# Retention, PReLU layer and routed experts in one kernel: a shift of float64 low bits moves from VectorE to ScalarE, and the planner counts other durations

## The chip, the cores and the metric

One NeuronCore of a Trainium2 chip runs the whole program. It has five engines that this document speaks of: TensorE (PE, and PEld for its weight loads), VectorE (DVE), ScalarE (ACT), GpSimd (POOL) and SyncE (SP, which issues most transfers). Each engine takes its instructions strictly in the order in which they were issued to it. The metric is the device time of one execution in microseconds (us).

## The reference, cut to what matters

Three layers follow one another. The sizes are 4 sequences of 768 tokens, 8 heads of 64 columns, so 3072 tokens of 512 columns.

```
state = gamma[h] * state + k_t v_t^T          # retention, per head; y_t = q_t state / sqrt(64)
h = x @ w_in                                  # 512 x 2048
g = max(h, 0) + alpha * min(h, 0)
x = (g @ w_out).astype(float32)               # 2048 x 512
logits = unit(x) @ unit(expert_emb).T / tau   # 8 experts, the best one is taken
out = gate * (max(x @ w1[e], 0) @ w2[e])      # 512 x 1024 and 1024 x 512
```

`w_in` and `w_out` are float64, because the draw of float32 numbers is multiplied by `1.0 / np.sqrt(...)` of NumPy's float64. The kernel gets them as the 64-bit patterns that they are.

## The kernel before, in words

**Tiles and stages.** A token tile is 128 tokens; there are 24, tile i being chunk i // 4 of sequence i % 4. Four tiles form a block. Products are done in float16 halves (a value is split into a high and a low half, and three products replace one), scaled by powers of two. The program has these stages:

1. The start: retention of tiles 0 to 7, the float64 weights `w_in` to float32 and then to halves.
2. The hidden layer of block 0 (`mm1(0, m)` for 16 values of m), and beside it the rest of `w_in`, all of `w_out`, and retention of four more tiles.
3. A long loop over steps: for each block the second product of the layer (`mm2`), the next block's `mm1`, the remaining retention tiles, the routing of finished tiles, and the splitting of the experts' weights into halves that go back to DRAM (`half_load`, `half_scale`, `half_pair`).
4. The routed experts' layer, slot by slot of 128 tokens of one expert.

**The conversion.** `convert(w, g, src)` turns a pair of chunks, 128 x 1024 float64 numbers, into float32. There are 16 pairs, eight of `w_in` and eight of `w_out`. A pair lands in one of three buffers that are used in turn (`f64_ring`, two parts of `f64_buf` and one of `pay_buf`), as pairs of 32-bit words, or four 16-bit words `h[:, :, 0..3]` a number, lowest first. On this follow:

- ScalarE multiplies the high word, read as a float32, by 2^-112 into `x`.
- VectorE shifts `h[:, :, 1]` right by 13 and writes the three bits into `h[:, :, 0]`.
- VectorE takes the sign out of `h[:, :, 3]` and writes it into `h[:, :, 1]`.
- VectorE shifts the bits of `x` left by 3 and puts in the low 32-bit word `f[:, :, 0]`, which now holds the sign and the three bits.
- ScalarE squares `x` and adds it up (`square_sum`), with the buffer `f` as the place for the squares, which nobody reads. After that the buffer takes the next pair.

The sums of squares give the scales, and `quarter(q)` and `split_out(g)` split the float32 chunks into halves on ScalarE and on VectorE or GpSimd in turn.

**The order of the work.** The kernel's text does not set the order directly. A class `Plan` records every instruction, with what it reads and writes, an engine and a duration in ns from `cost()`. `issue()` then works out, back from the end, by when each one is needed, plays the program through with these durations and the hand-over times of `AFTER`, and lets each engine take, of the instructions that are ready, the one that is needed first. The order found so is what is issued, on all five engines. It is fixed when the program is built; nothing of it is decided on the chip. Every recorded instruction is called at one line, 145, so most rows of the trace have that line, and the tiles tell them apart.

The changed lines are in `cost()` (lines 158 to 181 before) and `convert()` (lines 619 to 636).

Of the kernel before, what the change touches and what calls it, by code (L numbers as in the profile page):

```python
# [12 lines left out]
I32 = mybir.dt.int32  # L13
U16 = mybir.dt.uint16
AF = mybir.ActivationFunctionType
# [5 lines left out]
E, F = 8, 1024  # L21
P = 128
NCH = S // P              # chunks of a sequence
NTILE = NT // P           # token tiles: tile i is chunk i // B of sequence i % B
BT = B                    # token tiles of a block: one chunk of each sequence
# [4 lines left out]
NPRE = 2                  # tiles of the expert that has most tokens before the last block  # L30
NMIN = NTILE - NPRE       # the other tiles of tokens sorted by expert, at least
NSLOT = NMIN + E - 1      # and at most
SL = 30
CAP = NT                  # rows of an expert's region
PW = DM + 2               # words of a routed token: hi | lo | gate | id
# [3 lines left out]
# Powers of two that bring a norm into [2^(C-190.5), 2^(C-189.5)).  # L39
# [6 lines left out]
# columns of the float32 constants  # L46
# [11 lines left out]
def _constants():  # L58
# [23 lines left out]
    # decay of a query and of a key, by chunk: [c, (h2 d), 2, pair, t]  # L82
# [13 lines left out]
class Plan:  # L96
    """Records instructions in the order in which they would be right one after the other, and
    issues them in one in which each engine always takes, of the instructions whose operands are
    there, the one that is needed first. An instruction's place in the tensor engine's own
    sequence, and what waits for it, say when it is needed."""  # L100

    # from the end of an instruction to the start of another that waits for it; a DMA's issue
    # and its transfer are apart
    AFTER = {"PE": 197.0, "ACT": 145.0, "DVE": 140.0, "POOL": 100.0, "SP": 0.0}
    DMA_DONE, DMA_RATE = 940.0, 360.0
    COLD = 1500.0, 3500.0        # the tensor engine's idle time after which it is slow, and for how long
    SLACK = 8000.0
    PATIENCE = 0.7, 2000.0
    AHEAD = 60000.0          # how long before it is needed a DMA may be issued
    BACKLOG = 2500.0         # of DMA, beyond which none is issued  # L110

    def __init__(self, nc):
        self.nc = nc
        self.nodes = []
        self.log = {}            # reads and writes of a tensor: (region, node)
        self.unit_ = None
        self.pe_time = 0.0
        self.bias = 0.0
        self.vector = self.Engine(self, nc.vector, "DVE")
        self.scalar = self.Engine(self, nc.scalar, "ACT")  # L120
        self.gpsimd = self.Engine(self, nc.gpsimd, "POOL")
        self.tensor = self.Engine(self, nc.tensor, "PE")
        self.sync = self.Engine(self, nc.sync, "SP")
# [9 lines left out]
    class Engine:  # L133
# [23 lines left out]

        def cost(self, method, kw):
            """Engine's time, time until the result is there, bytes moved."""
# [16 lines left out]
            if self.name == "ACT":  # L176
                return 30.0 + 0.9 * n + (90.0 if kw.get("accum_out") is not None else 0.0), 0.0, 0
            if self.name == "DVE":
                fast = method in ("tensor_scalar", "tensor_copy") and n > 64
                return 65.0 + n * (0.52 if fast else 1.05), 0.0, 0  # L180
# [48 lines left out]
    def unit(self, eng):  # L229
        """Instructions of one engine that stay together."""  # L230
# [16 lines left out]
    def issue(self):  # L247
# [19 lines left out]
        while True:  # L267
# [16 lines left out]
            # rather wait a little for what is needed earlier  # L284
# [35 lines left out]
def retention_prelu_moe_kernel(ctx: ExitStack, tc, qkv, w_in, w_out, alpha, emb, tau, w1, w2,  # L320
# [17 lines left out]
    class Ring:  # L338
        """Buffers used in turn."""
# [28 lines left out]
    # A matrix in float32 lies two chunks of 512 columns behind the place where its halves go,  # L368
    # so that a pair's halves never land on what is still to be split.
    win = buf("win", [KF + 2, 512])  # L370
    wout = buf("wout", [KF + 2, 512])
    stage = buf("stage", [16, 512])         # experts' weights; before, halves of g
    xT = [buf(f"xT{k}", [2, KD, BW], F16) for k in range(2)]
    st_bd = buf("st_bd", [B, KD, P])
    f64_buf = buf("f64_buf", [4, 512, 2], I32)   # float64 weights; later, halves of g
# [7 lines left out]
    # the first chunk's tiles use what else waits for w_out  # L383
# [34 lines left out]
    def pow2(ss, s, c, hb=None):  # L418
        """Powers of two by which vectors of squared norm ss are scaled, into s."""
# [10 lines left out]
    def total(acc, n):  # L430
        """Sum of acc over partitions and columns, on every partition."""
        ps = m_ring.next()
        T.matmul(out=ps[:, 0:n], lhsT=ones32, rhs=acc, start=True, stop=True)
        t = tmp("tot", [1])
        V.tensor_reduce(out=t, in_=ps[:, 0:n], axis=AX.X, op=ALU.add)
        return t
# [4 lines left out]
    def norm(ss, n, e):  # L441
        """Newton's steps on 1/sqrt; 1e-6 on top of the norm."""
# [15 lines left out]
    def split(hi, lo, src, s, pool):  # L458
        """Halves of a pair of chunks. For the Pool engine the chunks are scaled first."""
# [21 lines left out]
    def att_hat(i):  # L481
        """Decayed queries and keys of tile i."""
# [11 lines left out]
    def att_a(i):  # L494
        """Masked scores of tile i."""
        hat = att[i]
        ring = x_ring if i < B + N_EARLY else m_ring
        # heads of one half of the partitions share a bank
# [14 lines left out]
    # From tile HALVED on, scores and values go into their product as halves.  # L513
# [8 lines left out]
    def att_s(i):  # L522
        """Halves of the scores and values of tile i; the state, scaled as their product is."""
# [27 lines left out]
    def att_b(i, early=False):  # L551
        """Outputs of tile i, the state after it, the halves of x."""
# [48 lines left out]
    def att_x(i, src):  # L601
        """The halves of x with the model dimension on partitions."""
# [4 lines left out]
    # The exponent is rebased by a product that moves the high word's upper eight exponent  # L607
    # bits, which takes what is too small for float32 to zero.
# [4 lines left out]
    s_in = buf("s_in", [KD])        # a scale for every quarter of w_in's columns  # L613
    i_in = buf("i_in", [KD])
    s_g = buf("s_g", [KD])          # what the halves of w_out's rows of a quarter are scaled by
# [3 lines left out]
    def convert(w, g, src):  # L619
        """Pair g of chunks to float32."""  # L620
        f = f64_ring.next()
        # w_in's chunks in the order of its columns
# [8 lines left out]
        # the low word becomes the sign and the three bits that the high word's shift makes room for  # L631
        h = f.rearrange("p n t -> p (n t)").bitcast(U16).rearrange("p (n t) -> p n t", t=4)
        V.tensor_scalar(out=h[:, :, 0], in0=h[:, :, 1], scalar1=13, scalar2=None, op0=ALU.logical_shift_right)
# [4 lines left out]
    def alpha_bound():  # L638
        # |g| <= |h| sqrt(1 + sum over partitions of their largest alpha^2)
# [7 lines left out]
    def quarter(q):  # L647
        """Halves of a quarter of w_in's columns."""
# [88 lines left out]
    class Route:  # L737
# [7 lines left out]
        def halve(self, o, acc):  # L745
            """A routed token's row: the halves of x scaled, its gate, where it is from."""
# [24 lines left out]
        def finish(self):  # L771
# [6 lines left out]
            # 1 / scale of the row; over the norm, for the logits  # L778
# [14 lines left out]
            # the first of the largest  # L793
# [7 lines left out]
            # ranks  # L801
# [17 lines left out]
            # gates  # L819
# [39 lines left out]
    g16 = {}  # L859

    def mm1(j, m):
# [11 lines left out]
        if j == 0:  # L873
            # the Pool engine takes a part while the vector engine has most to do
# [32 lines left out]
    # slots: the two tiles known early, what there is at least, what there may be  # L907
# [41 lines left out]
    def gather(t):  # L949
# [4 lines left out]
        # with the model dimension on partitions  # L954
# [78 lines left out]
    LAG = 0, 2, 4, 5          # of a tile's second layer in the last block  # L1033
# [52 lines left out]
    # the first slot's tokens  # L1086
# [11 lines left out]
    # the tiles that are left  # L1098
# [3 lines left out]
    # tiles of experts up to each one  # L1102
# [5 lines left out]
    # even slots take tiles from the first on, odd slots from the last back  # L1108
# [29 lines left out]
    # where a slot has no token, one that surely is there is read in its place, and nothing written  # L1138
# [8 lines left out]
    # expert of each slot; whether its weights have to be loaded  # L1147
# [11 lines left out]
    # 1 / (S_w1 S_w2) of each slot  # L1159
# [16 lines left out]
    def load_w(t):  # L1176
        """Weights of a slot, or of the two early ones. A slot's stay for the next but one of the same expert."""
        for piece in range(4):
# [3 lines left out]
            if t in (0, 1):  # L1182
                # the first of all tiles, and the last
# [93 lines left out]
def _arrange(inputs):  # L1277
    """The inputs as the chip loads them: each partition's share of a load in one run."""
    q, k, v = inputs["q"], inputs["k"], inputs["v"]

    def by_dim(a):      # [b, h, s, d] -> [(c b), (h2 d), (pair t)]
# [3 lines left out]
    def by_token(a):    # [b, h, s, d] -> [(c b), t, (h d)]  # L1285
# [5 lines left out]
    def rows(a):        # [.., (k p), f] -> [.., p, (k f)]  # L1291
# [4 lines left out]
    def in_chunks(a):  # L1296
# [5 lines left out]
        # float64, handed over as the bits that it is  # L1302
# [29 lines left out]
```

## Time and profile before

| | |
|---|---|
| median of 3 runs | 1041.25 us (1040.83 to 1045.32) |
| profiled execution, span from first to last instruction | 1051.0 us (its time with what lies around the span is not listed) |
| mean granted TensorE clock | 0.960 of full |
| busy, share of the span | PE 90%, PEld 53%, DVE 54%, ACT 47%, POOL 29% |
| instructions | 19041 |
| moved by the DMA engines | 201.45 MB, mean 192 GB/s |

The profiled execution is one execution, with its own start and end; its span is compared with stretches of its own trace, and the runs with one another. "Busy" is the time that an engine spends in instructions other than waits, branches and the issue of transfers. The page cuts the span into 40 slices of 26.3 us and gives the busy share of each in tenths (9 is 90% or more). A wait is put down to the instruction that came last of those it waited for.

### The profile page before, as it was taken

Reading aid. Unit: us, or ns where it says so; the run is one execution under the profiler, and the core shown is the slowest. Engines: PE = TensorE matmul, PEld = TensorE weight load, DVE = VectorE, ACT = ScalarE, POOL = GpSimd, SP = SyncE. Lnnn points to the kernel's source line nnn. Section 1 sums busy time; section 2 is a strip of 40 time slices with the busy share of each in tenths; the row PEclk is TensorE's granted clock in tenths of the full one; section 3 lists DMA queues with packets and bytes.
Section 4 is the critical chain, followed back from the end, with each engine's and each line's share of the span. In section 5 each row is a group of like instructions: output and inputs, shape, how many; then the busy total and the mean of one; then the engine's idle time right before and its main releaser. Section 6 shows DMA issues by size and latency. Waiting matters only on the chain. (4 is left out here: it accounts for less than half of the span.)

```text
span 1051.0 us, 19041 instructions
## 1 busy us (share of the span) xinstructions
PE 943.4 (90%) x7100; PEld 561.8 (53%) x7100; DVE 570.0 (54%) x1299; ACT 492.6 (47%) x865; POOL 304.0 (29%) x316
## 2 busy tenths in 40 slices
PE   5778876999999988988999899899889999998995
PEld 5664543555554544444444444444677777775763
DVE  5999999546766775567345554645712222221231
ACT  1457666546767956787667658742101010100100
POOL 1234556312342433323312321440231212113110
PEclk9887788999999989999999999999999999999998
DMA  8986532463866956876476557569575399825670
GB/s 279 307 268 193 189 129 71 114 188 91 234 197 197 251 151 213 240 201 191 171 220 164 187 181 214 157 219 316 186 201 168 72 292 315 243 65 132 151 287 21
DMA packets 129824, 201.45 MB, mean 192 GB/s; under 512 B 89726, under 2 KB 90110, under 8 KB 124608
## 3 DMA queue, kind: packets, MB, share of 16 engines
q1 hardware_dynamic: 123168, 179.42, 58.1%
q0 software_dynamic: 6560, 20.77, 5.8%
q8 instruction: 57, 0.93, 0.4%
q14 instruction: 39, 0.32, 0.1%
HBM read 204.59 MB, written 51.14 MB: 243 GB/s over the span
## 5 line engine op out<-in xcount | busy, mean ns | idle before, releaser
L145 PE MATMUL bank<-xT,win 128*128 128x512 f16 (+1 forms) x2208 | 338.9, 310 | 14.5 <-ACT g L145 7.3
L145 PEld LDWEIGHTS <-win 128*128 128x128 f16 x2400 | 186.8, 100 | 153.8 <-issue 31.9
L145 PE MATMUL bank<-wout,f_buf 128*128 128x512 f16 x960 | 227.5, 384 | 5.6 <-DVE pay_buf L145 4.8
L145 PEld LDWEIGHTS <-f_buf 128*128 128x128 f16 x960 | 92.9, 99 | 115.6 <-issue 11.4
L145 ACT ACTIVATE stage<-stage 128x1024 f16<-128x1024 f32 x96 | 101.0, 1052 | 54.9 <-DMA wsplit<-stage 46.0
L145 POOL TENSOR_TENSOR stage<-stage 128x1024 f16<-128x1024 f32 x32 | 68.2, 2131 | 146.1 <-ACT stage L145 117.8
L145 DVE SCALAR_TENSOR_TENSOR f_buf<-g,f_buf 128x512 f16<-128x512 f32 x80 | 72.7, 909 | 53.1 <-ACT f_buf L145 52.9
L145 DVE SCALAR_TENSOR_TENSOR g<-g,oma,bank 128x512 f32<-128x512 f32 x80 | 59.4, 744 | 73.5 <-ACT g L145 73.3
L145 ACT ACTIVATE st_bd<-bank 128x512 f16<-128x512 f32 x30 | 17.9, 597 | 149.7 <-PE bank L145 129.6
L145 POOL DMA_INDIRECT out<-xT,ids x25 | 25.3, 1013 | 214.4 <-DVE xT L145 181.5
L145 ACT ACTIVATE stage<-stage,se 128x1024 f16<-128x1024 f32 (+1 forms) x64 | 71.6, 1139 | 11.2 <-DVE se L145 6.5
L145 POOL TENSOR_TENSOR hat_buf<-qk_buf,cqk_sb 128x512 f32<-128x512 f32 x32 | 46.4, 1452 | 83.4 <-DMA qk_buf<-in_qkv 44.9
L145 PEld LDWEIGHTS <-wout 128*128 128x128 f16 x1152 | 65.5, 98 | 7.8 <-issue 4.8
L145 ACT ACTIVATE g<-bank 128x512 f32<-128x512 f32 x96 | 55.9, 584 | 26.0 <-PE bank L145 25.9
L145 PE MATMUL bank<-xT,wout 128*128 128x128 f16 x1056 | 62.7, 219 | 3.5 <-issue 3.4
L145 ACT ACTIVATE f_buf<-g 128x512 f16<-128x512 f32 x80 | 49.8, 622 | 34.1 <-DVE g L145 34.1
L145 PEld LDWEIGHTS <-st_bd 128*128 128x128 f16 x408 | 39.7, 99 | 45.3 <-issue 1.6
L145 DVE SCALAR_TENSOR_TENSOR st_bd<-bank,st_bd 128x512 f16<-128x512 f32 x34 | 23.5, 690 | 65.7 <-ACT st_bd L145 58.5
L145 DVE TENSOR_SCALAR xT<-bank,f_buf,cqk_sb 128x512 f32<-128x512 f32 x22 | 17.8, 809 | 67.0 <-PE bank L145 67.0
L145 PE MATMUL bank<-win,st_bd 128*128 128x512 f16 x216 | 49.4, 386 | 0.0
L145 PE MATMUL bank<-wout,stage 128*128 128x512 f16 (+1 forms) x208 | 48.8, 388 | 0.0
L145 DVE SCALAR_TENSOR_TENSOR stage<-stage,se 128x1024 f16<-128x1024 f32 x32 | 41.1, 1283 | 12.4 <-ACT stage L145 11.0
(253 smaller groups left out, 1320.9 us busy)
## 6 DMA issues: line engine op xcount, KB each, us to landing
win<-wsplit SPq DMA_DIRECT2D x56, 1024.0 KB
wout<-wsplit SPq DMA_DIRECT2D x52, 1024.0 KB
stage<-in_w SPq DMA_DIRECT2D x64, 512.0 KB
wsplit<-stage SPq DMA_DIRECT2D x64, 512.0 KB
qk_buf<-in_qkv SPq DMA_DIRECT2D x18, 768.0 KB
f_buf<-in_w_in SPq DMA_DIRECT2D x12, 512.0 KB
vp_buf<-in_qkv SPq DMA_DIRECT2D x20, 256.0 KB
f_buf<-in_w_out SPq DMA_DIRECT2D x10, 512.0 KB
```

Source lines behind the costliest of these rows:

```text
L145: call = lambda: fn(**kw)
```

## The change

In `convert`, ScalarE writes the three bits instead of VectorE, as a number: the 16-bit word times 2^-13, plus 2^-14 - 0.5, which rounded to an integer is the word shifted right by 13. The result is written as a whole 32-bit word, so that `h[:, :, 1]` is cleared by it, and VectorE's next step, which writes the sign there, comes after it. In `cost()` the durations of ScalarE and VectorE change. ScalarE's depend on where the input lies and on operands that are columns in memory; VectorE's no longer count operations on bits as fast ones, and count long instructions with two inputs 15% longer. Comments and docstrings go as well.

```diff
@@ cost()
+        BITS = (ALU.logical_shift_right, ALU.logical_shift_left, ALU.bitwise_and, ALU.bitwise_or)
+
         def cost(self, method, kw):
...
             if self.name == "ACT":
-                return 30.0 + 0.9 * n + (90.0 if kw.get("accum_out") is not None else 0.0), 0.0, 0
+                extra = sum(93.0 for k in ("accum_out", "scale", "bias") if isinstance(kw.get(k), bass.AP))
+                return (95.0 if kw["in_"].space != bass.MemoryType.PSUM else 50.0) + 0.833 * n + extra, 0.0, 0
             if self.name == "DVE":
-                fast = method in ("tensor_scalar", "tensor_copy") and n > 64
-                return 65.0 + n * (0.52 if fast else 1.05), 0.0, 0
+                fast = method in ("tensor_scalar", "tensor_copy") and n > 64 and kw.get("op0") not in self.BITS
+                two = method in ("scalar_tensor_tensor", "tensor_tensor") and n > 256
+                return 65.0 + n * (0.52 if fast else 1.05) * (1.15 if two else 1.0), 0.0, 0
             return 140.0 + (2.13 if method == "tensor_tensor" else 1.3) * n, 0.0, 0
@@ convert()
         A.activation(out=x, in_=f[:, :, 1].bitcast(F32), func=AF.Copy, scale=2.0 ** -112)
         h = f.rearrange("p n t -> p (n t)").bitcast(U16).rearrange("p (n t) -> p n t", t=4)
-        V.tensor_scalar(out=h[:, :, 0], in0=h[:, :, 1], scalar1=13, scalar2=None, op0=ALU.logical_shift_right)
+        A.activation(out=f[:, :, 0], in_=h[:, :, 1], func=AF.Copy, scale=2.0 ** -13, bias=2.0 ** -14 - 0.5)
         V.tensor_scalar(out=h[:, :, 1], in0=h[:, :, 3], scalar1=0x8000, scalar2=None, op0=ALU.bitwise_and)
         V.scalar_tensor_tensor(out=b, in0=b, scalar=3, in1=f[:, :, 0], op0=ALU.logical_shift_left, op1=ALU.bitwise_or)
```

## Rows read from the trace of the kernel before

**Rows 1.** The page: busy us by engine, then busy tenths in 40 slices.

```profile
PE 943.4 (90%) x7100; PEld 561.8 (53%) x7100; DVE 570.0 (54%) x1299; ACT 492.6 (47%) x865; POOL 304.0 (29%) x316
...
PE   5778876999999988988999899899889999998995
...
DVE  5999999546766775567345554645712222221231
```

**Rows 2.** Windows: stretch, length, busy us of each engine, granted clock, DMA share, GB/s.

```profile
20.00:181.00 161.00, 124.27 (x748) 84.85 (x748) 155.54 (x215) 95.57 (x156) 74.06 (x47) 0.85 0.63 193
...
20.00:80.00 60.00, 45.16 (x328) 38.30 (x327) 57.34 (x87) 29.07 (x50) 17.83 (x12) 0.88 0.88 262
...
181.00:1051.00 870.00, 809.12 (x6295) 467.68 (x6294) 404.75 (x1064) 394.08 (x707) 227.56 (x263) 0.98 0.64 188
240.00:700.00 460.00, 427.80 (x2493) 210.50 (x2492) 271.95 (x642) 323.46 (x574) 145.37 (x183) 0.98 0.65 193
400.00:500.00 100.00, 89.42 (x573) 45.77 (x572) 61.47 (x152) 74.29 (x138) 32.22 (x38) 0.98 0.72 206
500.00:600.00 100.00, 94.36 (x484) 43.44 (x482) 48.12 (x105) 65.12 (x106) 24.20 (x33) 1.00 0.63 186
```

**Rows 3.** Waits of VectorE, 20 to 181 us: total us, times, longest.

```profile
DVE hbx L145 <- ACT wout L145: 1.5, 3, 0.6
DVE g L145 <- ACT g L145: 1.2, 1, 1.2
DVE st_bd L145 <- PE bank L145: 0.8, 1, 0.8
```

**Rows 4.** Waits of TensorE, 20 to 181 us.

```profile
PE bank L145 <- DVE xh L145: 10.1, 3, 6.5
...
PE bank L145 <- ACT g L145: 7.3, 2, 6.6
```

**Rows 5.** Waits of ScalarE, 20 to 181 us.

```profile
ACT stage L145 <- DVE g L145: 14.9, 9, 2.9
```

**Rows 6.** VectorE's groups, 20 to 181 us: busy us, mean ns, idle before.

```profile
L145 DVE TENSOR_SCALAR f_buf<-f_buf 128x1024 uint16<-128x1024 uint16 x22 | 34.6, 1573 | 0.1
...
L145 DVE TENSOR_SCALAR pay_buf<-pay_buf 128x1024 uint16<-128x1024 uint16 x10 | 16.9, 1693 | 0.0
```

**Rows 7.** Timeline of VectorE: start us, duration us, instruction.

```profile
52.03 1.30 DVE L145 TENSOR_SCALAR pay_buf<-pay_buf 128x1024 uint16<-128x1024 uint16 x1
53.12 1.35 DVE L145 TENSOR_SCALAR f_buf<-f_buf 128x1024 uint16<-128x1024 uint16 x1
54.28 1.34 DVE L145 TENSOR_SCALAR pay_buf<-pay_buf 128x1024 uint16<-128x1024 uint16 x1
...
71.03 2.37 DVE L145 TENSOR_SCALAR pay_buf<-pay_buf 128x1024 uint16<-128x1024 uint16 x1
```

**Rows 8.** Timeline of GpSimd at the same time.

```profile
70.81 3.57 POOL L145 TENSOR_TENSOR hat_buf<-qk_buf,cqk_sb 128x512 f32<-128x512 f32 x2 [0.25 <-DMA cqk_sb<-in_cqk]
```

**Rows 9.** Timeline of ScalarE.

```profile
47.70 1.15 ACT L145 ACTIVATE win<-pay_buf 128x1024 f32<-128x1024 f32 x1
48.73 0.69 ACT L145 ACTIVATE wout<-bank,sx 128x512 f16<-128x512 f32 x1
```

**Rows 10.** ScalarE's groups, 20 to 181 us.

```profile
L145 ACT ACTIVATE win<-f_buf 128x1024 f32<-128x1024 f32 x6 | 6.8, 1132 | 0.0
...
L145 ACT ACTIVATE win<-win,s_in 128x1024 f16<-128x1024 f32 x4 | 4.6, 1146 | 3.7 <-DVE s_in L145 3.7
...
L145 ACT ACTIVATE win<-win 128x1024 f16<-128x1024 f32 x4 | 4.2, 1057 | 4.3 <-DVE win L145 4.3
```

**Rows 11.** One tile, `f_buf`: duration ns min/median/max, first and last start.

```profile
L145 SPq DMA_DIRECT2D f_buf<-in_w_in x12: 327/328/572, 6.8 to 97.0; - x12
...
L145 ACT ACTIVATION_READ_ACCUMULATOR f_buf<-wout x5: 186/187/221, 70.7 to 156.9; 128x1 f32 x5
```

**Rows 12.** Groups of the whole span: VectorE's costliest.

```profile
L145 DVE SCALAR_TENSOR_TENSOR f_buf<-g,f_buf 128x512 f16<-128x512 f32 x80 | 72.7, 909 | 53.1 <-ACT f_buf L145 52.9
```

## The prediction

> **What bounds the kernel now.** I read the page first: TensorE is busy for 90% of the span, VectorE for 54%, ScalarE for 47% [rows 1]. These are averages over two different stages, as the 40 slices show: in slices 2 to 7 VectorE stands at 9 tenths or more and TensorE at 6 to 8, and from slice 8 on it is the other way round [rows 1]. So the second view is the table of windows [rows 2]. From 20 to 181 us VectorE is busy for 155.5 of 161 us (97%), TensorE for 124.3, so it is idle for 36.7 us, and ScalarE for 95.6, so idle for 65.4. From 181 us to the end TensorE is busy for 809.1 of 870 us and VectorE for less than half.
>
> The third view says who waits for whom between 20 and 181 us. VectorE waits for 1.5, 1.2 and 0.8 us, and that is all [rows 3]. TensorE waits most for VectorE (10.1 us for the halves of x in xh), and the 7.3 us that are put down to ScalarE's g [rows 4] lie behind VectorE too, because ScalarE itself stands 14.9 us in front of its copies of g until VectorE has made them [rows 5]. So in this stage VectorE sets the end, and it has no gap left. The page's chain of what ended last tells only of the end of the kernel and is of no help here. All 16 conversions of float64 pairs lie in this stage, with 32 VectorE instructions on 128x1024 16-bit words [rows 6].
>
> The runs listed have a median of 1041.25 us; the profiled execution has a span of 1051.0 us, 9.75 us (0.9%) above it, and what lies around that span is not listed by itself. I make the sum on the profiled execution and take the difference over to the median unscaled.
>
> **The change part by part.** *Removed: 16 shifts on VectorE.* The two groups of 16-bit instructions hold 34.6 and 16.9 us in 32 instructions, 1.61 us each, and half of them go: 25.8 us by their durations [rows 6]. That is the upper bound. Two such instructions in a row start 1.09 and 1.16 us apart though each lasts 1.3 (at 52.03, 53.12 and 54.28 us) [rows 7], because the end of one overlaps the start of the next; 16 x 1.1 = 17.6 us is the lower bound. Most of the rest is waiting beside GpSimd: the one at 71.03 us lasts 2.37 us [rows 7] while GpSimd runs two products from 70.81 to 74.38 us [rows 8]. Whether such a wait goes with the instruction or falls on the next one is open. Of the excess, 51.5 - 32 x 1.31 = 9.6 us, half belongs to the shifts; I let half of that go: 17.6 + 2.4 = 20 us off VectorE.
>
> *A rule that speaks against the change.* The trace has VectorE at 1.1 us per 1024 words between starts [rows 7], and ScalarE at 1.03 us, from 47.70 to 48.73 us, for a copy that reads the same buffer [rows 9]: the two are level. The Trainium skill (ScalarE: Activation LUTs, section Rules for kernel authors) would keep a multiply or an add on VectorE, up to about three times as fast per element there. If that held, a shift would be worth some 0.35 us, the relief an estimated 16 x 0.35 = 5.6 us, and the result 1036 us at best. The row decides against it, since these words lie four apart and pass at about one in 1.07 ns, so this gets no chance of its own.
>
> *Two readings of the port.* VectorE's instruction is lengthened beside GpSimd's [rows 7, 8]. The Trainium skill (SBUF — State Buffer, section Who interferes with whom) lets those two share a pair of ports that one instruction holds to its end, with ScalarE never waiting for anyone. By it the moved instruction leaves the lock for good, and the sum would go by the 25.8 us instead of 20: some 1020 us.
>
> *Added: 16 products on ScalarE.* The trace has none with 16-bit input and 32-bit output at this stride. The nearest row is the copy that reads the same buffer with the same step, 1.13 us; a dense one takes 1.06 us [rows 10]. Below, 16 x 1.06 = 17 us; above, if the strided write cost as much again as the whole, 16 x 2.1 = 34 us. I take 1.13, 18.1 us in all. They lie in ScalarE's 65.4 idle us of the stage and leave 47, so I cost them at nothing; if that cover were gone they would cost their 18 us.
>
> *Added: a wait.* Before, VectorE could do both 16-bit steps as soon as a pair had landed. Now the mask writes the halfword that the product reads, so it waits for ScalarE, 16 times, and everything behind it on VectorE (the masked scores, g, the halves of x) waits too, since the order is fixed, and TensorE behind that. Lower bound 0, where the product comes early enough; upper bound 16 times the longest wait of VectorE for ScalarE in the stage, 1.2 us, 19 us. The ordinary wait of that kind is 0.5 us (1.5 in three) [rows 3]; with two thirds of the masks caught by one I take 5 us.
>
> *Held buffers.* The pairs go through three buffers. The first load is issued at 6.8 us and the last square sum over a pair is read at 156.9 us [rows 11]; 16 pairs on three buffers are 5.33 turns, so a turn lasts about 28 us, most of it queueing on VectorE, which shrinks with VectorE's load. I cost nothing, and a rival stands on the opposite. The DMA engines are busy for 0.88 of the time from 20 to 80 us, 0.63 over the stage [rows 2]; no long wait of VectorE is for a load [rows 3], so this costs nothing in the forecast, though it caps what the first 60 us can gain.
>
> *The planner's durations.* They add and remove no instruction; they change the order on every queue, SP's and GpSimd's too. A bit operation on 1024 columns counted 597 ns and counts 1140 (traced 1.1 us between starts); a two-input one on 512 counted 603 and counts 683; a scaled copy of 1024 on ScalarE counted 952 like an unscaled one and counts 1041, and the trace has 1146 against 1057 for these [rows 10]. In the first stage the plan had taken VectorE for lighter than it is by 32 x 0.5 = 16 us. For the stage that TensorE bounds I can only bound the effect. TensorE's busy time in two neighbouring windows of 100 us with the same loops is 89.4 and 94.4 us [rows 2], 5 us apart, so plus or minus 2.5 us in 100; over the 460 us from 240 to 700 that is 11.5 us either way. I take 0, having no row for a direction.
>
> *Sum.* 20 us off VectorE, less 5 us of new waits, takes 15 us off the stage from 20 to 181 us, which then lasts 146. TensorE's 124.3 busy us fit into that (85%). Its granted clock, 0.85 over the stage [rows 2], may rise when its gaps shrink; as VectorE sets the stage I count nothing for it. What follows is bound by TensorE and simply begins 15 us earlier: span 1036, and for the runs 1041.25 - 15 = **1026 us**. What is late next is still VectorE, up to about 166 us.
>
> **The rivals.** *The new hand-over eats the relief.* The masks wait about 1 us each, near the longest that VectorE now waits, and the waits beside GpSimd fall on other instructions: 17.6 - 16 = 1.6 us gained, 1039 to 1040 us. For it: the two engines already wait for one another in turn, 14.9 us before the copies of g alone [rows 5]. Against it: ScalarE is idle for two fifths of the stage.
>
> *The order gets worse where TensorE bounds.* The 15 us come, and 11.5 are lost again from 240 to 700 us: 1038 us. For it: every queue is reordered, by numbers of which the two-input one (683 ns) still misses the 909 ns of its costliest group [rows 12]. Against it: the new numbers are mostly nearer to the rows.
>
> *The three buffers become the bound; slower than before.* A turn needs one more ScalarE step in series (1.03 us and a hand-over of some 0.2), and that step stands in ScalarE's fixed order behind instructions that wait for VectorE, up to 2.9 us each (14.9 us in 9 waits is 1.7 on average) [rows 5]. The relief is worth 3 x 1.1 = 3.3 us a turn. From about 2 us of such queueing for each pair on, a turn is longer than before; at 4 us it is 1.03 + 0.2 + 4 - 3.3 = 1.9 us longer, 5.33 turns give 10 us, and the time is 1051 us. For it: the serial chain. Against it: the 28 us of a turn are mostly queueing on the engine that is relieved.
>
> *The new durations help beyond the first stage.* 15 and most of 11.5 us: 1016 us or less.
>
> **How the numbers follow.** Forecast 0.60 (1017 to 1034 by itself), hand-over 0.10, worse order 0.10, buffers 0.12, more than forecast 0.08. The range reaches from 25.8 us of relief with no new wait and half of the planner's gain (1041.25 - 25.8 - 5.5 = 1010) to a little above no change (1043), which takes in the two middle rivals with a small loss. About 0.5% (5.2 us) is what a measurement of this kernel tells from no change. Faster by more than that: the forecast, the larger gain and 0.04 of the worse order, whose loss may be smaller, 0.72; within it: the rest of the two middle rivals, 0.16; slower: 0.12.
>
> **What would show it.** After: 16 instead of 32 16-bit instructions on VectorE; 16 new ones on ScalarE of about 1.13 us; VectorE's saturated stretch ends near 166 us instead of 181, with some 5 us more of waits for ScalarE in it; from there on windows with the same busy TensorE as before, shifted. The forecast is wrong if VectorE's stretch ends as late as before with gaps in it (hand-over, or buffers if the gaps lead back to loads), if it ends earlier but TensorE is idle for clearly more than the 32.2 us that it is from 240 to 700 us [rows 2] over the same work (worse order), or if the new products last 2 us.

## The result, and the profile after

The changed kernel takes 1031.44 us (median of 4 runs, 1030.72 to 1034.24) against 1043.28 us of the kernel before beside it: a ratio of 0.9891, 95% interval 0.986 to 0.9922. That is 11.4 us off 1041.25, where 15 were forecast.

The page after has TensorE at 92% of a span of 1029.1 us. Its first lines, and the slices of TensorE, VectorE and ScalarE (slices of 25.7 us):

```profile
PE 941.7 (92%) x7100; PEld 566.3 (55%) x7100; DVE 546.2 (53%) x1283; ACT 507.5 (49%) x881; POOL 299.6 (29%) x316
...
PE   5798787999998999989899999998879999999995
...
DVE  5888877566757875575346545645722222222231
ACT  1668887356767877785567668642101011110100
```

VectorE's row of nines in slices 2 to 7 [rows 1] has become eights and sevens, and ScalarE stands at 8 in slices 4 to 6. No engine is full over the whole first stage any more; TensorE has one nine there, in slice 3, and nines in a row only from slice 8 on. VectorE has 16 instructions fewer than before, ScalarE 16 more.

Where the time went has to be read at the same point of the work, not at the same time. I use two marks that every trace has: the first and the last high half of `g` of blocks 1 to 5 that ScalarE writes (`f_buf<-g`, 80 of them). They cut the span into the first stage, the loop that TensorE bounds, and the rest. The windows of the changed kernel from 20 us to the first mark, between the marks, and after them (columns as in [rows 2]):

```profile
20.00:216.60 196.60, 168.42 (x1044) 111.74 (x1044) 153.13 (x260) 132.95 (x213) 82.77 (x57) 0.88 0.62 187
...
216.60:697.80 481.20, 456.61 (x2644) 225.92 (x2642) 286.98 (x667) 335.99 (x597) 152.74 (x188) 0.98 0.67 197
697.80:1029.10 331.30, 306.97 (x3359) 219.48 (x3357) 96.25 (x335) 35.95 (x69) 61.70 (x64) 0.97 0.65 190
```

The same three of the trace of the kernel before:

```profile
20.00:227.80 207.80, 167.28 (x1043) 109.72 (x1043) 179.19 (x276) 117.03 (x196) 88.43 (x57) 0.87 0.59 178
...
227.80:717.80 490.00, 457.80 (x2645) 224.37 (x2644) 285.34 (x667) 336.73 (x598) 151.40 (x188) 0.98 0.66 195
717.80:1051.00 333.20, 308.32 (x3359) 218.44 (x3357) 95.76 (x335) 35.88 (x69) 61.79 (x64) 0.98 0.64 187
```

The counts of VectorE's instructions up to the first mark are 276 and 260, so for VectorE the two windows hold the same work but for the 16 shifts. VectorE's busy time there falls by 26.1 us, the stage by 11.2. The loop is 8.8 us shorter. The first trace of the kernel before had, however, a span (1051.0 us) some 10 us above the median of its runs and longer than any of them, so a second one was needed (the first experiment).

### The profile page after: what moved, and what is told of

Same layout as the page of the kernel before. It is cut to its first block, busy times and chain, and to the rows that moved or that the text cites. A ratio compares the mean times of both kernels' runs of the same rounds, so it can differ in the third digit from the quotient of the medians.

```text
span 1029.1 us, 19040 instructions
## 1 busy us (share of the span) xinstructions
PE 941.7 (92%) x7100; PEld 566.3 (55%) x7100; DVE 546.2 (53%) x1283; ACT 507.5 (49%) x881; POOL 299.6 (29%) x316
## 5 line engine op out<-in xcount | busy, mean ns | idle before, releaser
L145 PE MATMUL bank<-wout,f_buf 128*128 128x512 f16 x960 | 227.0, 384 | 2.0 <-DVE pay_buf L145 1.8
```

What stands on the lines that cost most here:

```text
L145: call = lambda: fn(**kw)
```

## The experiments

Three sets of kernels ran, each beside the kernel before on the same chip; its medians there were 1040.13, 1041.12 and 1049.51 us. Ratios are therefore compared, not times; the changed kernel itself is in none of the three sets, its ratio is the one of the result above. First mark and loop are each from one trace of the kernel.

| kernel | median us | ratio, 95% interval | first mark us | loop us |
|---|---|---|---|---|
| before, first and second trace | | 1 | 227.8, 226.1 | 490.0, 486.5 |
| changed | 1031.44 | 0.9891 (0.986 to 0.9922) | 216.6 | 481.2 |
| e1 product only | 1035.88 | 0.9959 (0.9935 to 0.9983) | 222.6 | 484.1 |
| e2 durations only | 1045.22 | 1.0064 (1.0038 to 1.0089) | 233.4 | 478.2 |
| e3 changed, masks twice | 1050.60 | 1.0100 (1.0065 to 1.0135) | 239.0 | 480.8 |
| e4 before, no shift | 1025.80 | 0.9832 (0.9806 to 0.9857) | 211.7 | 487.1 |
| e5 changed, no product | 1026.65 | 0.9866 (0.9845 to 0.9887) | 213.3 | 478.9 |
| e6 changed, old ScalarE durations | 1035.34 | 0.9940 (0.992 to 0.9959) | 218.8 | 484.8 |
| e7 changed, no 15% | 1021.86 | 0.9811 (0.979 to 0.9832) | 215.2 | 476.1 |
| e8 product, slow bit operations | 1039.59 | 0.9918 (0.9886 to 0.9949) | 213.5 | 485.0 |
| e9 product, ScalarE durations | 1032.93 | 0.9842 (0.9806 to 0.9878) | 217.4 | 477.9 |
| e10 changed, 14% | 1026.05 | 0.9781 (0.9753 to 0.9809) | 213.6 | 471.2 |
| e11 changed, 8% | 1031.60 | 0.9830 (0.9802 to 0.9857) | 215.5 | 476.6 |

**e0: the kernel before again.** No edit.

> The kernel before once more, for a second trace. Both theories: 1041 to 1045 us. What is asked of the trace is how much of the 21.9 us between the two profiled spans (1051.0 and 1029.1) belongs to the one execution and not to the kernel: I expect a span of 1040 to 1043 us, the end of the conversions near 157 us as in the first trace, and the missing 10 us in the loop that TensorE bounds, from the first high half of g of block 1 (227.8 us) to the last of block 5 (717.8 us), 490 us in the first trace.

One run, 1037.95 us, span 1036.2, both below what I expected. Its windows:

```profile
20.00:226.10 206.10, 168.59 (x1042) 113.92 (x1043) 176.84 (x276) 116.92 (x195) 90.10 (x57) 0.87 0.58 179
...
226.10:712.60 486.50, 458.21 (x2645) 225.27 (x2644) 283.79 (x668) 336.95 (x598) 150.06 (x188) 0.98 0.66 196
712.60:1036.20 323.60, 304.37 (x3359) 217.83 (x3357) 96.12 (x335) 35.89 (x69) 61.78 (x64) 0.98 0.67 193
```

I had the place wrong: 1.7 us of the difference lie in the first stage, 3.5 in the loop and 9.6 behind it. Against the mean of the two traces the change takes 10.4 us off the first stage (227.0 to 216.6) and 7.1 off the loop (488.3 to 481.2), and the rest is 2.9 us longer. That rest moves by more than this from one execution of one kernel to the next, so I draw nothing from it.

**e1 and e2: each half of the change alone.**

```diff
e1, on the kernel before
-        V.tensor_scalar(out=h[:, :, 0], in0=h[:, :, 1], scalar1=13, scalar2=None, op0=ALU.logical_shift_right)
+        A.activation(out=f[:, :, 0], in_=h[:, :, 1], func=AF.Copy, scale=2.0 ** -13, bias=2.0 ** -14 - 0.5)
e2, on the changed kernel: the same two lines the other way round
```

> Only the product on ScalarE; the planner keeps its old durations. Theory A (VectorE's load in the first 181 us is what counts): 10 to 15 us faster than before, ratio 0.986 to 0.990, as much as the whole change. Theory B (the gain is the new order that the planner's durations give): within 3 us of before. Theory C (the old durations count the removed shift at 597 ns only and the added product at 952, so the plan sees no relief and puts the product badly): 3 to 8 us faster.

> Only the planner's durations; the shift stays on VectorE. Theory A: within 3 us of before, since VectorE has as much to do as before. Theory B: 8 to 12 us faster, ratio 0.988 to 0.992, nearly all in the loop that TensorE bounds. Theory C: 3 to 8 us faster.

The product alone brings 0.41%, the durations alone cost 0.64%, and the two together bring 1.09%. Theory A fails for e1 by its size, C has that size right, and all three fail for e2. Up to the first mark e1, then e2:

```profile
20.00:222.60 202.60, 169.69 (x1046) 113.79 (x1045) 156.51 (x260) 133.05 (x212) 83.77 (x57) 0.87 0.60 182
```

```profile
20.00:233.40 213.40, 169.84 (x1043) 115.70 (x1043) 181.07 (x276) 117.59 (x196) 89.50 (x57) 0.86 0.56 172
```

In e1 VectorE is busy for 21.5 us less than in the kernel before (178.0, the mean of two) and only 4.4 us of it come out. In e2 it has the same work as before and needs 6.5 us more for it: it is busy for 3.1 us more (181.1 against 178.0) and idle for 3.4 us more. Nothing but the order differs there. From e2 to the changed kernel, the product under the new durations, the mark moves by 16.8 us and the ratio by 1.7%.

**e3: the load given back, the order kept.**

```diff
         V.tensor_scalar(out=h[:, :, 1], in0=h[:, :, 3], scalar1=0x8000, scalar2=None, op0=ALU.bitwise_and)
+        plan.nodes[-1].calls.append(plan.nodes[-1].calls[-1])
```

> The changed kernel in its own order, but each of the 16 masks on VectorE is issued twice, so VectorE has its 16 instructions of 1.1 us (17.6 us) back, without any wait of its own. If VectorE still sets the end of the first stage (theory A), 9 to 16 us slower than the changed kernel, back to 1040 to 1047 us. If the relief has made something else late there (ScalarE, the three buffers or TensorE), 0 to 5 us slower than the changed kernel, 1031 to 1036 us.

2.1% slower than the changed kernel, more than expected. Up to the mark:

```profile
20.00:239.00 219.00, 173.52 (x1045) 117.39 (x1045) 177.60 (x276) 133.07 (x212) 88.23 (x57) 0.86 0.55 168
```

VectorE is busy for 24.5 us more and the stage takes 22.4 us more. So VectorE still sets the end of the first stage of the changed kernel, though it is busy for only 153.1 of its 196.6 us. If it were only each pair's way through its buffer that got longer, a third of the 24.5 us would have come, some 8 us (an estimate: three buffers hold three pairs side by side).

**e4 and e5: the shift and the product left out, the orders kept.**

```diff
e4, on the kernel before
         V.tensor_scalar(out=h[:, :, 0], in0=h[:, :, 1], scalar1=13, scalar2=None, op0=ALU.logical_shift_right)
+        plan.nodes[-1].calls.clear()
e5, on the changed kernel
         A.activation(out=f[:, :, 0], in_=h[:, :, 1], func=AF.Copy, scale=2.0 ** -13, bias=2.0 ** -14 - 0.5)
+        plan.nodes[-1].calls.clear()
```

> The kernel before with its order unchanged on every engine, but the 16 shifts on VectorE are left out and nothing takes their place, so the low halfword keeps 16 bits of the float64 instead of three. Theory A (VectorE's load in the first stage is the price, 1 to 1): 12 to 20 us faster than before, 1021 to 1028 us. Theory D (an order that was made for a VectorE with the shifts turns most of the relief into new waits of VectorE, as with the product alone, where 21 us less of busy VectorE brought 4 us): 3 to 8 us faster, 1032 to 1037 us.

> The changed kernel with its order unchanged on every engine, but the 16 products on ScalarE are left out, so the three bits and the cleared halfword are missing and the mask waits for nobody. What the product and the hand-over cost. If they lie in ScalarE's idle time (my sum without the 5 us of waits): within 2 us of the changed kernel, 1029 to 1033 us. If the hand-over costs VectorE the 5 us that I put into the sum: 1025 to 1028 us. If ScalarE with 51 of 60 us busy between 80 and 140 us sets the pace there: 1020 us or less.

Up to the mark, e4 and then e5:

```profile
20.00:211.70 191.70, 164.87 (x1044) 109.22 (x1043) 156.26 (x260) 117.00 (x196) 88.79 (x57) 0.89 0.63 192
```

```profile
20.00:213.30 193.30, 163.49 (x1043) 108.42 (x1043) 154.25 (x260) 117.15 (x196) 87.73 (x57) 0.89 0.64 190
```

e4 is theory A: 1.68% (17.5 us of 1041) without the shifts, in the old order. Of 21.8 us less of busy VectorE 15.3 come out at the mark. e5 says what the product and its hand-over cost in the changed kernel: 3.3 us at the mark, 0.25% by the ratios, whose intervals overlap. By its time, 1026.65 us, the hand-over theory holds; by the ratio the cost lies between that theory and nothing. ScalarE does not set the pace.

**e6 to e9: which duration does it.**

```diff
e6, on the changed kernel
-                extra = sum(93.0 for k in ("accum_out", "scale", "bias") if isinstance(kw.get(k), bass.AP))
-                return (95.0 if kw["in_"].space != bass.MemoryType.PSUM else 50.0) + 0.833 * n + extra, 0.0, 0
+                return 30.0 + 0.9 * n + (90.0 if kw.get("accum_out") is not None else 0.0), 0.0, 0
e7, on the changed kernel
-                return 65.0 + n * (0.52 if fast else 1.05) * (1.15 if two else 1.0), 0.0, 0
+                return 65.0 + n * (0.52 if fast else 1.05), 0.0, 0
e8: the edits of e6 and e7 together
e9: the edit of e7, and on the changed kernel
-                fast = method in ("tensor_scalar", "tensor_copy") and n > 64 and kw.get("op0") not in self.BITS
+                fast = method in ("tensor_scalar", "tensor_copy") and n > 64
```

> The changed kernel with VectorE's new durations but ScalarE's old ones in the planner. If it is VectorE's durations that the product needs (theory E: the plan must know that bit operations are slow, so that it sees VectorE as the late engine): within 3 us of the changed kernel, 1028 to 1034 us. If it is ScalarE's (the product is put well because scaled copies are known to be long): 1036 to 1045 us.

> The changed kernel, its planner without the 15% on long instructions with two inputs. If the 15% is what shortens the loop that TensorE bounds (by 5 to 9 us between the first and the last high half of g of blocks 1 to 5 in the three kernels that have the new durations): 1036 to 1041 us, with that loop at 484 to 490 us and the first stage as in the changed kernel, 217 us. If the loop comes from another term: within 3 us of the changed kernel, loop 478 to 481 us.

> The product on ScalarE, and of the planner's new durations only that bit operations on VectorE are slow (597 to 1140 ns); ScalarE's old durations, no 15%. Theory E (what the product needs is a plan that knows VectorE's bit operations): most of the first stage's gain is there, first high half of g of block 1 at 216 to 219 us, and the loop stays as before at 484 to 488 us: 1029 to 1035 us. Theory F (the gain belongs to ScalarE's durations): first stage as with the product alone, 222 us: 1034 to 1039 us.

> The product on ScalarE, and of the planner's new durations only ScalarE's. Theory E: first stage near the product alone, 220 to 223 us, the loop shorter at 476 to 480 us: 1027 to 1033 us. Theory F: first stage at 215 to 217 us and the loop at 476 to 480 us, 1020 to 1025 us, as without the 15% alone.

The loop answers plainly. In the eight kernels whose plan has ScalarE's new durations it lasts 471.2 to 481.2 us (mean 477.6), in the six traces whose plan has the old ones 484.1 to 490.0 (mean 486.3), and the two groups do not touch. They hold six orders and four (e3 and e5 keep the changed kernel's order, e4 that of the kernel before), and within each of the three sets those with the new durations have the shorter loop. So ScalarE's durations take about 9 us off the loop, on the mean, and VectorE's do not. The marks of the changed kernel, of e8 and of e9, from the rows of the tile `g` (duration ns, first and last start):

```profile
L145 ACT ACTIVATE f_buf<-g x80: 612/627/631, 216.6 to 697.8; 128x512 f16<-128x512 f32 x80
```

```profile
L145 ACT ACTIVATE f_buf<-g x80: 612/621/631, 213.5 to 698.5; 128x512 f16<-128x512 f32 x80
```

```profile
L145 ACT ACTIVATE f_buf<-g x80: 612/620/632, 217.4 to 695.3; 128x512 f16<-128x512 f32 x80
```

The first stage gives no such answer: with the product it ends anywhere from 213.5 to 222.6 us in eight orders (mean 216.7), with slow bit operations in the plan (e8) or without them (e9). Neither theory E nor theory F describes that: taken over by ratio to 1041 us, e8 comes to 1033 us as E has it and e9 to 1025 us as F has it, but the first mark of e8 is earlier than E allows and that of e9 a little later than F allows. e6 lies between its two expectations. And e7 fell outside both of its expectations: taking the 15% away made the kernel faster, 0.9811, not slower or the same.

**e10 and e11: how finely the order hangs on a duration.**

```diff
-                return 65.0 + n * (0.52 if fast else 1.05) * (1.15 if two else 1.0), 0.0, 0
+                return 65.0 + n * (0.52 if fast else 1.05) * (1.14 if two else 1.0), 0.0, 0
e11: 1.08 in its place
```

> A control on how finely the order hangs on the durations: the changed kernel with 14% instead of 15% on long instructions with two inputs, 7 ns less on 683. If the effect of a duration is a matter of its size: within 1.5 us of the changed kernel, 1030 to 1033 us. If a greedy order turns small differences into different orders of a few us either way (theory L, for luck): anywhere from 1022 to 1040 us, and then the 9.5 us that the 15% cost must not be read as the price of that term.

> The changed kernel with 8% instead of 15%. If the 15% costs by its size, about half of the 9.5 us between 0% and 15% is back: 1025 to 1028 us. Theory L: anywhere from 1020 to 1040 us, with no order between 0, 8, 14 and 15%.

0, 8, 14 and 15% give 0.9811, 0.9830, 0.9781 and 0.9891: no order in them, and 14% and 15%, which differ by 5 ns in 683 (not the 7 that I wrote), lie 1.1% apart with intervals that do not meet. These two ratios come from two sets of runs, though, and by plain times, 1026.05 and 1031.44 us, the two kernels are only 0.5% apart. In the set that e10 is of, e8 to e11, the stretch behind the loop is longer than in all other traces (336.0 to 338.8 us against 323.6 to 333.2), and why is not shown. So I compare the work up to the end of the loop. The row of e10 beside that of the changed kernel above has a loop 10 us shorter and a first mark 3 us earlier:

```profile
L145 ACT ACTIVATE f_buf<-g x80: 612/629/631, 213.6 to 684.8; 128x512 f16<-128x512 f32 x80
```

The loop ends 13.0 us earlier than in the changed kernel (684.8 against 697.8 us), where two traces of the kernel before are 5.2 us apart (712.6 and 717.8). That is theory L, though by its ratio (1018 us of 1041) e10 is even below the range that I gave it. One order is a draw. In the five orders with the product and ScalarE's new durations the loop ends between 684.8 and 697.8 us; less the scatter of single traces, a draw is worth some 5 us either way in this kernel (an estimate). What e7 gained must not be read as the price of the 15%, nor what e2 lost as that of the durations. e7 and e10 both beat the changed kernel and the kernel before, by ratio and by plain time; e10 has the best ratio of all, e7 the lowest time.

## Why the prediction was right, and where it was not

**VectorE bounds the first stage.** Shown from both sides: e4 takes 21.8 us off VectorE and 15.3 off the stage, e3 puts 24.5 on and 22.4 come.

**The relief.** 20 us forecast; by the mean of the two traces before, 178.0 us of busy time became 153.1, 24.9 us. That is nearly the upper bound of 25.8: the waits beside GpSimd went with the shifts and hardly fell on others, since the rest of VectorE's work, 178.0 less 25.8, is 152.2 us before and 153.1 after; the prediction's second reading of the port had that, but the 1020 us that it gave did not come. In the old order less went: without the shifts 156.3 us are left (e4), 4 us more than 152.2. The 16 masks that stayed, in the changed kernel (20 to 181 us), last 1.59 us on average as the 32 did [rows 6]:

```profile
L145 DVE TENSOR_SCALAR f_buf<-f_buf 128x1024 uint16<-128x1024 uint16 x11 | 16.3, 1477 | 3.6 <-ACT f_buf L145 3.6
...
L145 DVE TENSOR_SCALAR pay_buf<-pay_buf 128x1024 uint16<-128x1024 uint16 x5 | 9.2, 1834 | 0.7 <-ACT pay_buf L145 0.7
```

**The product.** 1.13 us and 18.1 in all forecast; measured 1.15 and 1.14, 12.6 + 5.7 = 18.3 us, so the strided 32-bit write costs next to nothing beyond the strided read [rows 10]:

```profile
L145 ACT ACTIVATE f_buf<-f_buf 128x1024 int32<-128x1024 uint16 x11 | 12.6, 1149 | 0.0
...
L145 ACT ACTIVATE pay_buf<-pay_buf 128x1024 int32<-128x1024 uint16 x5 | 5.7, 1139 | 0.0
```

Beside GpSimd it isn't lengthened. At 134.4 us a product starts beside an instruction of GpSimd and lasts 1.13 us, and a mask that starts then lasts 2.06 (timeline of the changed kernel: start us, duration us):

```profile
134.44 1.04 POOL L145 TENSOR_TENSOR hat_buf<-qk_buf,cst 128x512 f32<-128x512 f32 x1 [0.35 <-PE bank L145]
134.47 1.13 ACT L145 ACTIVATE pay_buf<-pay_buf 128x1024 int32<-128x1024 uint16 x1
134.60 2.06 DVE L145 TENSOR_SCALAR f_buf<-f_buf 128x1024 uint16<-128x1024 uint16 x1 [0.68 <-ACT f_buf L145]
```

The tile `f_buf` has the products between 1124 and 1172 ns and the masks between 1309 and 2209 (min/median/max):

```profile
L145 ACT ACTIVATE f_buf<-f_buf x11: 1124/1153/1172, 20.8 to 135.5; 128x1024 int32<-128x1024 uint16 x11
L145 DVE TENSOR_SCALAR f_buf<-f_buf x11: 1309/1332/2209, 26.7 to 139.9; 128x1024 uint16<-128x1024 uint16 x11
...
L145 ACT ACTIVATION_READ_ACCUMULATOR f_buf<-wout x5: 185/186/227, 67.8 to 146.7; 128x1 f32 x5
```

The Trainium skill (SBUF — State Buffer, section Who interferes with whom) says that ScalarE never waits for anyone's port; these rows agree.

**The hand-over.** 5 us forecast, 3.6 + 0.7 = 4.3 us of waits measured in the two rows of masks above, and e5 puts the whole of product and hand-over at 3.3 us of the stage. Right, as far as one trace of each tells.

**The step that was mis-sized** is the one from relief to time: "20 us off VectorE, less 5 us of new waits, takes 15 us off the stage". VectorE's busy time fell by 24.9 us and the stage by 10.4, so 14.5 us became idle time of VectorE, not 5. The waits of VectorE in the changed kernel, 20 to 181 us (total us, times, longest):

```profile
DVE hbx L145 <- ACT wout L145: 4.7, 4, 1.8
DVE hbx L145 <- ACT xh L145: 4.4, 2, 3.8
DVE g L145 <- ACT g L145: 4.3, 2, 3.7
DVE f_buf L145 <- ACT f_buf L145: 3.6, 3, 2.1
DVE win L145 <- ACT win L145: 2.1, 3, 0.8
```

Only the fourth belongs to the masks. The others are old hand-overs, the scales of x (`hbx`), `g` and the halves of `w_in`, of which little showed while VectorE was late for everything [rows 3]. They do not come from the product: without it (e5, 20 to 170 us) they stand there too.

```profile
DVE hbx L145 <- ACT xh L145: 4.8, 3, 3.4
DVE g L145 <- ACT g L145: 4.3, 2, 3.7
DVE hbx L145 <- ACT wout L145: 3.5, 5, 1.1
DVE win L145 <- ACT win L145: 2.9, 3, 1.3
```

Nor does the first row of the list above need the new order: with the shifts left out of the old one (e4, 20 to 170 us) that wait is longer still.

```profile
DVE hbx L145 <- ACT wout L145: 6.7, 4, 2.3
```

How the 14.5 us split can be read from VectorE's idle time up to the first mark, the length of the window less the busy time: 28.6 and 29.3 us in the two traces before, 35.4 in e4, 32.3 in e2, 39.0 in e5 and 43.5 in the changed kernel. So some 6.5 us come to light in the old order when the shifts go (e4), some 3.4 come with the new order alone (e2), and some 4.4 with the product and its hand-over (from e5 to the changed kernel); each of these is a difference of single traces.

I had asked what is late next and answered "still VectorE". That is so for more load and only in part for less: e4 gave back 0.7 us for each us taken away, and the changed kernel, with another order and the product, 0.4.

**The planner's durations.** Costed at 0 with 11.5 us either way. Two things stood behind that zero. ScalarE's durations shorten the loop, by about 9 us on the mean of the orders tried; the draw of the order moves the whole by some 5 us either way (the estimate above) and gave the changed kernel the latest end of the loop of the five. Which instruction of the loop is better placed by ScalarE's durations is not shown: TensorE's idle time in it is 32.2 and 28.3 us in the two traces before and 24.6 after. The largest of its waits there, for ScalarE's `stage`, is nearly the same (11.3 us in the first trace before, 10.2 after); what went is spread over short waits for VectorE. So that what follows "simply begins 15 us earlier" was not right either: 10.4 us come from the first stage and 7.1 from the loop. That the total came near the 15 us forecast is in part luck: the stage gave 4.6 us less than the sum had, and the loop, which the sum had at nothing, gave 7.1, which as far as e6 to e9 tell come from ScalarE's durations and not from the moved shift.

**The rivals.** The three buffers did not become the bound: the last square sum over a pair of `f_buf` is read at 146.7 us (the row above) instead of 156.9 [rows 11]. The worse order in the loop did not come; the loop got shorter. Hand-over eating the relief describes the size of e1 (4.4 of 21.5 us), not the changed kernel; and in e1 too the masks wait for only 2.8 us (20 to 181 us), the rest being other waits of VectorE.

## What to carry to other kernels

Where one engine is full over a whole stage, moving work off it to an idle engine pays, but count only part of the relief (here 0.2 to 0.7 us a us, by the order), because hand-overs that its lateness hid come to light. Compare traces at the same point of the work, and take a second trace of the kernel before, to know by how much two executions of one kernel differ. Where a planner orders the instructions, vary its numbers by amounts that should not matter before crediting a change of them: here 14% for 15% was worth as much as the change by ratio, and half of it by plain time.

## What the runs showed of the hardware

After the loop two executions of one and the same kernel differ by 9.6 us (333.2 and 323.6). In the longer one TensorE's weight loads stand for 15.3 us, 18 times, for nothing that the profile names ("issue"); first trace of the kernel before, from 717.8 us:

```profile
PEld L145 <- issue: 15.3, 18, 5.7
```

and the second, from 712.6 us:

```profile
PEld L145 <- issue: 5.4, 1, 5.4
```

What the engine does in those gaps no run here shows, nor why the stretch behind the loop is longer in e8 to e11.
